# DeltaNet and gated MLP on one core: wider products in the triangular solve, later masks, another queue order and smaller first blocks in an inverse

## The chip, the cores and the metric

The kernel runs on one core of a Trainium2 chip. A core has a tensor engine (PE, matrix products into PSUM), VectorE (DVE), ScalarE (ACT), GpSimd (POOL) and SyncE (SP, which issues transfers). The metric is the device time of one execution in microseconds (us); lower is better. Times of one kernel are medians over several runs; the profile is of one further execution.

## The reference

A DeltaNet recurrence over 768 positions for 4 batches x 8 heads of width 48, and then a two-layer MLP with a sigmoid gate (384 to 2048 to 384) over the 3072 tokens:

```python
for t in range(S):
    kt, vt, bt = (k_n[:, :, t], v[:, :, t], beta[:, :, t, None])
    y[:, :, t] = np.einsum('bhd,bhde->bhe', q[:, :, t], state)
    v_old = np.einsum('bhde,bhd->bhe', state, kt)
    state = state + bt[:, :, :, None] * np.einsum('bhd,bhe->bhde', kt, vt - v_old)
...
h = x @ w_in
g = h * (1.0 / (1.0 + np.exp(-1.702 * h)))
return (g @ w_out).astype(np.float32)
```

Keys are divided by their norm first (`k_n`). The weights of the MLP arrive as 64-bit floats and are converted on the chip to 32-bit ones.

## The kernel before

**Chunks and units.** The recurrence is cut into 6 chunks of 128 positions (`C`), so that a unit is one chunk of one batch with its 8 heads: 24 units, numbered `n`, chunk by chunk. Units of different batches are independent; a chunk of a batch needs the state that the chunk before left.

**The solve in a unit.** Inside a chunk the 128 updates depend on each other through the Gram matrix G of the keys. The kernel splits the 128 rows into 4 blocks of 32 (`BS`, `NB`). `solve` multiplies the inverse of a diagonal block (XB) with the block's rows of V into psU; `solved` copies psU to the rows of U on ACT; `below` multiplies the Gram rows of the block with these U rows, for each later block of rows a product of its own (32 rows of contraction, 32 output rows, 48 columns), into psR; `rest` takes psR from the later rows of V on DVE, below block 0 in two instructions (rows 32 to 63, rows 64 to 127). Then the next block can be solved. `together` issues the products of one stage: for each head, the solves of one or two units and the belows of another, so that the chains of two or three units interleave.

**Order over the units.** Chunk 0 runs in two pairs of chains: `hops` names the stages of a pair, and the two loops over `2 * NB` stages in the kernel's end run them, with other work between: `fill(n)` converts n pieces of the MLP's weights on DVE, `preparing` (the generator `keys`) normalizes, transposes and multiplies the keys of the four units of chunk 1 and writes their diagonal blocks out, `warm` issues dense products whose results nobody reads, and `feed` issues MLP work. From chunk 1 on, `woven(n, share)` holds three stages, with unit n at blocks 1 and 2, unit n-1 at blocks 2 and 3 and unit n+1 at block 0: (solve n block 1, below n-1 block 2), (solve n-1 block 3 and n+1 block 0, below n block 1), (solve n block 2, below n+1 block 0). Between them `spend` issues MLP products (ph and po) on PE.

**Inverses.** `invert` inverts all diagonal blocks of a chunk (or of two of its batches) at once on DVE, one block per partition. It inverts two blocks of 16 rows (`HS`) inside each block of 32 by substitution, in 15 steps of one multiply and one reduction, and joins them by two products (`dots`). For chunk 0 it runs while the tensor engine prepares scores; for chunk 1 it takes turns with MLP work.

**Masks.** `select` zeroes the part of the scores M that lies on and below the diagonal, on GpSimd. For chunk 0 the four masks are issued behind the inverse's code in one loop; nothing in them waits for the inverse, so each starts when its M is there.

**Queues.** Instructions made by `vec`, `act`, `pe`, `pool`, `sync` and `other_queue` keep the order in which the program issues them on their engine. `sync` goes to SP's queue, `other_queue` to GpSimd's. In `prepare`, a unit of chunk 1 writes its four diagonal blocks to memory (Nd) and reads them back in another layout (NT), all on SP. Between the two pairs SP is also given the queries and values of units 4 and 5.

Of the kernel before, what the change touches and what calls it, by code (L numbers as in the profile page):

```python
# [18 lines left out]
def kernel(  # L19
# [274 lines left out]
    def fill(n):  # L294
        for _ in range(n):
            next(converting, None)
# [105 lines left out]
    def prepare(n):  # L402

        c, b = units[n]
        turn(n)
        yield 0.6
        G = gram(n)
        if c == 1:
            Nd = dram.tile([H * C * BS], F32, tag="Nd", name="Nd", bufs=4)
            for blk in range(NB):  # L410
                u = slice(blk * BS, (blk + 1) * BS)
                sync(out=Nd.rearrange("(h p k) -> p h k", p=C, k=BS)[u], in_=G[u, :, u])
            yield 0.9
            sync(
                out=NT[b * NB * H : (b + 1) * NB * H].rearrange("d i k -> d (i k)"),
                in_=Nd.rearrange("(d r) -> d r", r=BS * BS),
            )
            yield 0.0
            return
        Nd = dram.tile([H * NS], F32, tag="Nd", name="Nd", bufs=4)  # L420
        dma = sync if c < 3 else nc.sync.dma_start
        dma(
            out=Nd.rearrange("(h r) -> h r", r=NS)[:, 0 : C * C].rearrange(
                "h (p k) -> p h k", k=C
            ),
            in_=G,
        )
        dma(
            out=NT[b * NB * H : (b + 1) * NB * H],
            in_=Nd.rearrange("(d r) -> d r", r=NS // NB)[:, 0 : BS * C].rearrange(  # L430
                "d (i k) -> d i k", k=C
            )[:, :, 0:BS],
        )
        yield 0.9
# [6 lines left out]
    def invert(c, b0=0, nb=B):  # L441

        np = nb * NB * H
        part = slice(b0 * NB * H, b0 * NB * H + np)
        N, Y = NT[part], YB[part]
        bc = bI[part, c].broadcast_to([np, BS, BS])
        tt, red = vec.tensor_tensor, vec.tensor_reduce
        if c > 0:
            tt(N, N, bc, op=ALU.mult)
            yield 0.0  # L450
        HS = BS // 2

        def dots(o, a, b, ny, nx, nk, negate):

            P = wk.tile([128, ny, nx, nk], F32, tag="P", name="P")[part]
            tt(P, a, b, op=ALU.mult)
            red(o, P, axis=AX.X, op=ALU.add, negate=negate)

        def halves(t):

            return [t[:, s * HS : (s + 1) * HS, s * HS : (s + 1) * HS] for s in range(2)]


        Yf = Y.rearrange("p j i -> p (j i)")
        Nf = N.rearrange("p i k -> p (i k)")
        step = HS * BS + HS

        def diag(t, off, dims):
            return bass.AP(t.tensor, t.offset + off, [t.ap[0], [step, 2]] + dims)

        for i in range(1, HS):
            P = wk.tile([128, 2, i, i], F32, tag="P", name="P")[part]
            tt(
                P, diag(Nf, i * BS, [[0, i], [1, i]]), diag(Yf, 0, [[BS, i], [1, i]]),
                op=ALU.mult,
            )
            red(diag(Yf, i, [[BS, i]]), P, axis=AX.X, op=ALU.add, negate=True)
            yield 0.0


        X1 = N[:, 0:HS, HS:]
        if c <= 1:
            vec.tensor_copy(X1, halves(Y)[1].rearrange("p l i -> p i l"))
        else:
            act.activation(X1, halves(Y)[1].rearrange("p l i -> p i l"), ACT.Copy)
        A = N[:, 0:HS, 0:HS]
        N10, Y0 = N[:, HS:, 0:HS], halves(Y)[0]
        Q = 4
        for j in range(0, HS, Q):
            n = HS - j  # L490
            dots(
                A[:, j : j + Q, :],
                N10[:, :, j:].rearrange("p (o l) k -> p o l k", o=1).broadcast_to([np, Q, HS, n]),
                Y0[:, j : j + Q, j:].rearrange("p j (o k) -> p j o k", o=1).broadcast_to([np, Q, HS, n]),
                Q, HS, n, False,
            )
            yield 0.0
        for i in range(0, HS, Q):
            n = i + Q
            if c == 0 and i == HS - 3 * Q:  # L500
                warm(NY, vec.memset)
            dots(
                Y[:, 0:HS, HS + i : HS + i + Q],
                A[:, :, 0:n].rearrange("p j (o l) -> p j o l", o=1).broadcast_to([np, HS, Q, n]),
                X1[:, i : i + Q, 0:n].rearrange("p (o i) l -> p o i l", o=1).broadcast_to([np, HS, Q, n]),
                HS, Q, n, True,
            )
            yield 0.0
        if c == 0:
            T = wk.tile([128, BS, BS], F32, tag="P", name="YT")  # L510
            vec.transpose(T.rearrange("p d i -> p i d"), Y.rearrange("p j i -> p i j"))
            for b in range(B):
                XB = wk.tile([128, H, BS], F32, tag="XB", name="XB", bufs=4)
                tt(
                    XB, T[:, b * H : (b + 1) * H],
                    zs[:, 5, b].broadcast_to([128, H, BS]), op=ALU.mult,
                )
                inverse[b] = XB
                yield 0.0
            return  # L520
        YS = wk.tile([128, BS, BS], F32, tag="P", name="YS")[part]
        tt(YS, Y, bc, op=ALU.mult)
        dma = sync if c < 3 else nc.sync.dma_start
        groups = [range(b0, b0 + nb)]
        back = {}
        for bs in groups:
            for b in bs:
                back[b] = dram.tile([H * C, BS], F32, tag="Yd", name="Yd", bufs=4)
                dma(
                    out=back[b].rearrange("(p j) i -> p j i", j=BS),  # L530
                    in_=YS[(b - b0) * NB * H : (b - b0 + 1) * NB * H],
                )
            for b in bs:
                XB = wk.tile([128, H, BS], F32, tag="XB", name="XB", bufs=4)
                dma(out=XB, in_=back[b].rearrange("(h t) i -> t h i", h=H))
                inverse[c * B + b] = XB
        yield 0.0
# [7 lines left out]
    class Step:  # L545
# [63 lines left out]

        def below(self, blk, h, psR):  # L610
            r = slice(blk * BS, (blk + 1) * BS)
            for k in range(blk + 1, NB):
                u = slice(k * BS, (k + 1) * BS)
                pe.matmul(
                    psR[u, h, :], lhsT=self.G[r, h, u], rhs=self.U[r, h, :],
                    start=True, stop=True,
                )

        def rest(self, blk, psR):
            for u in (slice(BS, 2 * BS), slice(2 * BS, C)) if blk == 0 else (slice((blk + 1) * BS, C),):  # L620
                vec.tensor_tensor(self.V[u], self.V[u], psR[u], op=ALU.subtract)

        def solve(self, blk, h, psU):
            r = slice(blk * BS, (blk + 1) * BS)
# [328 lines left out]
    for s in pair:  # L953
        for h in range(H):
            act.mul(s.V[:, h, :], s.V[:, h, :], zs[:, 4, s.b, h : h + 1])
    for s in pair:
        s.select()

    def hops(a, b):
# [12 lines left out]
    def keys():  # L972

        def unit(n):
            yield from normalize_mixed(n)
            yield from prepare(n)

        begun[2 * B] = prepare(2 * B)

        def first(n):  # L980
            yield from normalize_mixed(n)
            next(begun[n])

        work = [unit(n) for n in range(B, 2 * B)] + [first(2 * B)]
        for t in range(22):
            for u, begin in enumerate((0, 3, 6, 10, 13)):
                s = t - begin
                if s >= 0 and s % 2 == 0:
                    next(work[u], None)
            yield  # L990
        for w in work:
            run(w)
# [2 lines left out]
    path = hops(*pair[:2])  # L995
    for i in range(2 * NB):
        together(*next(path))
        fill(1 if i < 2 else 2)
        if i > 0:
            ahead_of(preparing, 1)  # L1000
        warm(NU if i < 6 else NA)
    for n, s in enumerate(pair[:2]):
        put_out(s, 2 - n)
        load(len(KN) + n, ((KN, k),), other_queue)
        fill(1 + n)
    for n in range(B, B + 2):
        load(n, ((QP, q),), sync)
    for n in range(B, B + 2):
        load_values(n, sync)

    ffn = []

# [13 lines left out]
    for i in range(2 * NB):  # L1026
        together(*next(path))
        fill(2 if i < 5 else 3)
        if i > 2:
            feed()  # L1030
        else:
            warm(NU)
        ahead_of(preparing, 2)
        if 3 <= i < 6:
            fetch_out(i - 3)
    for s in pair[2:]:
        put_out(s, 2)
        feed()
        fill(1)
    ffn.append(hidden(xTs[1], gTs[1], slice(0, NTH), 1.3, True))  # L1040
    xTs.pop(0), xTs.pop(1)
    load(B + 2, ((QP, q),), sync)
    for n in range(2 * B + 1, 2 * B + 1 + HB):
        load(n, ((KN, k),), sync)
# [55 lines left out]
```

## Time and profile before

| what | us |
|---|---|
| median of 3 runs (lowest, highest) | 775.44 (774.95, 776.5) |
| the profiled execution, whole | 775.34 |
| its span in the profile | 773.6 |
| PE busy / PE weight loads busy | 747.1 / 560.1 |
| DVE / ACT / POOL busy | 455.2 / 241.5 / 126.5 |
| psU products: busy (records) | 68.6 (1536) |
| psR products: busy (records) | 60.0 (2208) |
| V minus psR on DVE: busy (instructions) | 53.3 (96) |

A product of 32-bit floats leaves two records (two passes) on PE, and weight loads are recorded apart from the products (PEld). Busy times of products that run beside each other are counted once. The mean duration of a product in the profile is its way through the pipeline (203 ns for psU and psR), not the distance to the next. The granted clock (PEclk) is the share of full speed that the tensor engine was given: 0.976 over the span. DMA and engine times in a stretch of the span are read from a table by stretch, and the order of single instructions from the timeline.

### The profile page before, as it was taken

How to read it: one execution, taken by the hardware profiler on the slowest of the kernel's cores; microseconds unless marked ns; L12 is line 12 of the kernel's file. 1: busy time of each engine (PE TensorE's matmuls, PEld its weight loads, DVE VectorE, ACT ScalarE, POOL GpSimd, SP SyncE). 2: the span in 40 equal slices, each digit the busy share in tenths (PEclk: the TensorE clock that was granted, in tenths of full speed). 3: DMA queues.
4: the chain of work that ended last, by engine and by line, in shares of the span. 5: the costliest groups of instructions: out<-in, count | busy, mean ns of one | idle time of the engine just before them, and what ended most of it. 6: DMA issues, size and time to landing. Idle time of an engine off the chain costs nothing.

```text
span 773.6 us, 18836 instructions
## 1 busy us (share of the span) xinstructions
PE 747.1 (97%) x8165; PEld 560.1 (72%) x8165; DVE 455.2 (59%) x935; ACT 241.5 (31%) x535; POOL 126.5 (16%) x132
## 2 busy tenths in 40 slices
PE   7898999789999999999999999999999999999997
PEld 6677788456688678678678678678678677686774
DVE  6989879996975675665665665666665621000000
ACT  4564642343333223223223233233223123121110
POOL 6314200010220320220221211221210000000000
PEclk8598999999999999999999999999999999999999
DMA  9946640644342142042042042042030020000000
GB/s 167 176 65 174 145 87 1 170 114 97 76 109 56 25 105 56 22 107 57 22 101 63 22 100 65 22 97 66 22 77 13 22 44 2 16 12 1 25 1 21
DMA packets 130658, 50.73 MB, mean 66 GB/s; under 512 B 105408, under 2 KB 126016, under 8 KB 130576
## 3 DMA queue, kind: packets, MB, share of 16 engines
q1 hardware_dynamic: 128112, 41.08, 24.5%
q0 software_dynamic: 2464, 8.46, 4.5%
q8 instruction: 64, 1.05, 0.6%
q14 instruction: 18, 0.15, 0.1%
HBM read 32.08 MB, written 16.25 MB: 62 GB/s over the span
## 4 chain that ended last, share of the span: by engine, by line
PE 80%; DVE 14%; issue 2%; DMA 2%; ACT 2%; SPq 0%; POOL 0%; DVEq 0%; POOLq 0%; ACTq 0%
PE po L102 29%; PE ph L102 26%; PE psY L102 6%; PE psU L102 5%; PE psQ L102 4%; PE psG L102 4%; PE psT L102 3%; DVE P L102 3%; DVE w_out L102 2%; DVE tmp L102 2%; DVE YB L102 2%; PE psR L102 2%; PE ps_warm L102 2%; DVE V L102 1%; DVE NT L102 1%
## 5 line engine op out<-in xcount | busy, mean ns | idle before, releaser
L102 PE MATMUL po<-w_out,gT 128*128 128x384 f32 x768 | 266.1, 494 | 7.4 <-DVE w_out L102 7.4
L102 PE MATMUL ph<-xT,w_in 128*128 128x256 f32 x1152 | 261.2, 383 | 0.3
L102 PEld LDWEIGHTS ph<-xT,w_in 128*128 128x128 f32 x1152 | 214.8, 190 | 32.6 <-issue 1.7
L102 PEld LDWEIGHTS po<-w_out,gT 128*128 128x128 f32 x768 | 141.1, 190 | 98.8 <-DVE w_out L102 9.1
L102 DVE TENSOR_TENSOR V<-V,psR 64x384 f32<-64x384 f32 (+1 forms) x96 | 53.3, 555 | 189.8 <-PE psR L102 186.8
L102 ACT ACTIVATE gT<-ph 128x512 f32<-128x512 f32 x96 | 56.5, 596 | 142.3 <-PE ph L102 142.2
L102 DVE TENSOR_TENSOR P<-NT,YB 64x8 f32<-64x8 f32 (+31 forms) x190 | 89.4, 470 | 5.4
L102 ACT COPY US<-psU 32x384 f32<-32x384 f32 x92 | 43.2, 470 | 134.7 <-PE psR L102 120.5
L102 DVE TENSOR_REDUCE YB<-P 64x4 f32<-64x8 f32 (+31 forms) x190 | 80.9, 426 | 6.5
L102 PEld LDWEIGHTS psU<-V,XB 32*32 32x32 f32 x1536 | 57.7, 105 | 36.5 <-issue 27.7
L102 PE MATMUL psU<-V,XB 32*32 32x48 f32 x1536 | 68.6, 203 | 3.2 <-DVE V L102 2.4
L605 POOL TENSOR_SCALAR_AFFINE_SELECT M<-M 128x1024 f32<-128x1024 f32 x20 | 25.4, 1268 | 231.4 <-DVE M L102 167.4
L102 PE MATMUL psR<-US,G 32*32 32x48 f32 x2208 | 60.0, 203 | 0.6 <-ACT US L102 0.6
L102 PEld LDWEIGHTS psR<-US,G 32*32 32x32 f32 x2208 | 50.7, 105 | 1.9 <-ACT US L102 0.7
L102 PE MATMUL psQ<-QS,kT 48*128 48x176 f32 (+1 forms) x384 | 37.6, 341 | 3.0 <-ACT QS L102 3.0
L102 PE MATMUL psG<-kT 48*128 48x128 f32 x384 | 32.4, 306 | 3.4 <-ACT kT L102 2.2
L102 PEld LDWEIGHTS psQ<-QS,kT 48*128 48x128 f32 x384 | 31.1, 209 | 6.2 <-ACT QS L102 5.1
L102 DVE TENSOR_TENSOR P<-NT 64x256 f32<-64x256 f32 (+7 forms) x40 | 34.3, 859 | 0.4
L102 DVE TENSOR_REDUCE NT<-P 64x64 f32<-64x1024 f32 (+7 forms) x40 | 32.6, 815 | 1.4
L102 PEld LDWEIGHTS psG<-kT 48*128 48x128 f32 x384 | 27.4, 205 | 6.8 <-ACT kT L102 2.6
L102 ACT COPY o<-po 128x384 f32<-128x384 f32 x24 | 11.5, 479 | 61.7 <-issue 39.2
L102 ACT COPY M<-psQ 128x256 f32<-128x256 f32 x68 | 22.8, 376 | 22.7 <-DVE V L102 16.0
(99 smaller groups left out, 600.9 us busy)
## 6 DMA issues: line engine op xcount, KB each, us to landing
Nd<-G SPq DMA_DIRECT2D x16, 512.0 KB, 3.5
QP<-in_q_dram SPq DMA_DIRECT2D x24, 192.0 KB, 4.3
V<-in_v_dram SPq DMA_DIRECT2D x24, 192.0 KB, 3.1
out_dram<-o SPq DMA_DIRECT2D x24, 192.0 KB, 2.6
KN<-in_k_dram POOLq DMA_DIRECT2D x15, 192.0 KB, 3.6
NT<-Nd SPq DMA_DIRECT2D x20, 128.0 KB, 2.6
Yd<-YS SPq DMA_DIRECT2D x20, 128.0 KB, 2.4
XB<-Yd SPq DMA_DIRECT2D x20, 128.0 KB, 3.3
```

Of the source, the lines that this page charges most:

```text
L102: return lambda *a, **kw: tc.keep_in_program_order(op(*a, **kw))
L605: (pool if self.n < B else nc.gpsimd).affine_select(out=self.M, in_=self.M, compare_op=ALU.is_gt, fill=0.0, base=0, pattern=[[0, H], [1, 1 ...
```

## The change

- `below`: one product for all rows below a block instead of one for each block of 32. Below block 0 it runs over all 128 output rows, below block 1 over rows 64 to 127, below block 2 over rows 96 to 127. `rest` is one subtraction over the same rows; below block 0 it also changes the rows of block 0 itself, which are not read again.
- `invert`: for chunks 0 and 1 the substitution goes over four blocks of 8 rows (7 steps), and pairs of them are joined by four `dots` of 8 x 8 x 8 after one copy.
- Masks of chunk 0: a copy on GpSimd that reads the last column of YB, which the inverse writes last, stands ahead of them; the first two masks follow it, and the other two are issued in the first pair's loop after stages 3 and 5.
- SyncE's order: an extra `yield` between the writes of Nd and the read of NT; `keys` steps the later units first, in 24 turns instead of 22; the queries and values of units 4 and 5 are loaded in the second pair's loop (stage 5) and behind it, no longer ahead of it. In the first two stages `fill` converts two pieces instead of one.

```diff
             for blk in range(NB):
                 u = slice(blk * BS, (blk + 1) * BS)
                 sync(out=Nd.rearrange("(h p k) -> p h k", p=C, k=BS)[u], in_=G[u, :, u])
+            yield 0.0
             yield 0.9
             sync(
                 out=NT[b * NB * H : (b + 1) * NB * H].rearrange("d i k -> d (i k)"),
...
-        for i in range(1, HS):
-            P = wk.tile([128, 2, i, i], F32, tag="P", name="P")[part]
+        for i in range(1, QS):
+            P = wk.tile([128, nb8, i, i], F32, tag="P", name="P")[part]
...
+        if QS < HS:
+            shape = [np, QS, QS, QS]
+            first, second = ([slice(s * HS + o, s * HS + o + QS) for s in range(2)] for o in (0, QS))
+            vec.tensor_copy(
+                diag(Nf, QS, [[BS, QS], [1, QS]], 2), diag(Yf, QS * BS + QS, [[1, QS], [BS, QS]], 2)
+            )
+            for a, b in zip(first, second):
+                dots(
+                    N[:, a, a],
...
+            for a, b in zip(first, second):
+                dots(
+                    Y[:, a, b],
...
         def below(self, blk, h, psR):
             r = slice(blk * BS, (blk + 1) * BS)
-            for k in range(blk + 1, NB):
-                u = slice(k * BS, (k + 1) * BS)
-                pe.matmul(
-                    psR[u, h, :], lhsT=self.G[r, h, u], rhs=self.U[r, h, :],
-                    start=True, stop=True,
-                )
+            u = self.under(blk)
+            pe.matmul(
+                psR[u, h, :], lhsT=self.G[r, h, u], rhs=self.U[r, h, :],
+                start=True, stop=True,
+            )
+
+        def under(self, blk):
+
+            return slice((blk + 1) * BS if blk else 0, C)
 
         def rest(self, blk, psR):
-            for u in (slice(BS, 2 * BS), slice(2 * BS, C)) if blk == 0 else (slice((blk + 1) * BS, C),):
-                vec.tensor_tensor(self.V[u], self.V[u], psR[u], op=ALU.subtract)
+            u = self.under(blk)
+            vec.tensor_tensor(self.V[u], self.V[u], psR[u], op=ALU.subtract)
...
-    for s in pair:
+    pool.tensor_copy(landed, YB[:, 0, BS - 1 : BS])
+    for s in pair[:HB]:
         s.select()
...
-        for t in range(22):
-            for u, begin in enumerate((0, 3, 6, 10, 13)):
+        for t in range(24):
+            for u, begin in reversed(list(enumerate((0, 3, 6, 10, 13)))):
...
-        fill(1 if i < 2 else 2)
+        fill(2)
+        if i in (3, 5):
+            pair[HB + (i - 3) // 2].select()
...
-    for n in range(B, B + 2):
-        load(n, ((QP, q),), sync)
-    for n in range(B, B + 2):
-        load_values(n, sync)
...
+        if i == 5:
+            load(B, ((QP, q),), sync)
+            load_values(B, sync)
...
+    load(B + 1, ((QP, q),), sync)
+    load_values(B + 1, sync)
```

## The prediction

> **What bounds the kernel now.** I read the slices of the span first, then the busy time by stretch, then the chain that ended last.
>
> ```profile
> PE   7898999789999999999999999999999999999997
> ...
> PEclk8598999999999999999999999999999999999999
> ...
> PE 80%; DVE 14%; issue 2%; DMA 2%; ACT 2%; SPq 0%; POOL 0%; DVEq 0%; POOLq 0%; ACTq 0%
> ```
>
> The tensor engine (PE) is full at full clock from slice 10 on and carries 80% of the chain; VectorE (DVE) carries 14%, all before 180 us.
>
> ```profile
> 44.00:64.00 20.00, 16.91 (x394) 13.77 (x395) 17.89 (x30) 8.59 (x19) 1.85 (x2) 0.92 0.28 51
> ...
> 120.00:180.00 60.00, 50.72 (x390) 33.83 (x389) 53.83 (x102) 20.97 (x41) 4.87 (x3) 0.97 0.41 104
> 180.00:774.00 594.00, 588.17 (x6202) 436.27 (x6200) 301.14 (x629) 160.03 (x353) 85.60 (x68) 1.00 0.20 48
> ```
>
> Columns: stretch, length, busy PE, PE weight loads, DVE, ScalarE, GpSimd, granted clock, DMA share, GB/s. From 180 us on PE is busy 588 of 594 us and DVE only 301: there a microsecond more of PE is a microsecond more of time, and one less of DVE is worth nothing. DVE is near its limit only between 44 and 180 us. So I price each edit on PE first.
>
> **How a stage of small products runs.** Weight loads around one `together` of chunk 1 (start, duration, engine, operation):
>
> ```profile
> 285.84 0.62 PEld L102 LDWEIGHTS ph<-xT,w_in 128*128 128x128 f32 x3
> 286.79 0.11 PEld L102 LDWEIGHTS psU<-V,XB 32*32 32x32 f32 x2 [0.33 <-issue]
> 286.81 0.11 PEld L102 LDWEIGHTS psR<-US,G 32*32 32x32 f32 x2
> ...
> 287.43 0.11 PEld L102 LDWEIGHTS psR<-US,G 32*32 32x32 f32 x2
> 287.61 0.51 PEld L102 LDWEIGHTS ph<-xT,w_in 128*128 128x128 f32 x3
> ```
>
> From 286.79 to 287.52 lie 8 heads, each with two passes (an f32 product is two records) of two psU and two psR. One pass of all four takes 42 ns (0.68 us over 16), just the stream of 48 columns; and a stage with one psU and three psR has the same period (294.79 to 295.39 us). The four run beside each other, each in its own 32x32 square: two of three psR cost nothing today.
>
> Around the stage the shape changes. The last ph of 128x128 starts at 286.487 and streams 213 ns, to 286.700; the next load waits until 286.794. At the far end the last psR starts at 287.478 and streams to 287.518; ph's load waits until 287.607. So 94 and 89 ns of nothing, and then a load that lies beside no product. I read the same gap at all 264 places of the trace where the shape changes: at least 89 to 110 ns for each of 16 pairs of shapes, also where the rows stay and only the columns change (psD 64x32 to psG 64x128: 94 ns). Between equal shapes there is none.
>
> **The Trainium skill.** "TensorEngine Tiling (Array Packing)", Key Properties, says that different tiles run in parallel and that "Changing tiling mode (not just tile) drains the TensorE", 32x32, 32x64 and 32x128 being different modes: the trace agrees, with those gaps. "TensorE: Matmul & The Clock Gate", LDWEIGHTS, has a load cost its columns over 1.2, whatever the rows: agreed, 48-column products on 64-column weights come every 58 ns (297.214 to 297.272), not every 42; so a 128-column load is about 107 ns. Its Part 1 says that the clock falls to half after a 3.4 us window with too little work; see below. "GPSIMD Engine Reference", Specifications: SBUF access shared with VectorE for instructions with two SBUF inputs.
>
> ```profile
> 33.49 0.42 DVE L102 TENSOR_TENSOR P<-NT,YB 128x256 f32<-128x256 f32 x1
> ...
> 34.19 1.09 POOL L102 TENSOR_SCALAR_AFFINE_SELECT M<-M 128x1024 f32<-128x1024 f32 x1 [1.97 <-ACT M L102]
> 34.40 1.16 DVE L102 TENSOR_TENSOR P<-NT 128x256 f32<-128x256 f32 x1
> ```
>
> It agrees once in four masks: the multiply took 1.16 us beside a mask, 0.42 alone.
>
> **The change part by part.**
>
> *One product.* Below block 0 it is 32x128 (rows 0 to 127, the first 32 unused), below block 1 32x64, below block 2 32x32 as before. `together` still alternates solve and below head by head, so wherever below 0 or 1 meets a solve, the shape changes twice a head. The trace has no 32x32 next to 32x128; I price by the gaps above. psU: gap 94, load 27, two passes 84: 205 ns. 32x128: gap 90, load 107, pass 42, and the second load, overlapping that pass, ends 107 after the first; pass 42: 347 ns. Head 552 ns, stage 4.42 us against 0.68: +3.7. 32x64: gap 90, two loads of 53 and a pass of 42: 238 to 248 ns, head 0.45 to 0.46 us, stage about 3.7 us: +3.0. In `woven`, below 1 meets solves in 20 steps and below 0 in 19; the first below 0 is alone (16 loads of 107 ns: +1.0). 19 x 3.7 + 1 + 20 x 3.0 = **+132 us**, all where PE is the bound. Chunk 0 has 4 + 4 such stages in its two pairs of chains, 27 us; PE idles 9 us between 120 and 180 us, some of which takes this up: **+20**.
>
> *The clock.* Windows of 3.41 us, and the one after each:
>
> ```profile
> 57.41:60.82 3.41, 1.90 (x41) 1.24 (x38) 3.28 (x7) 1.41 (x2) 0.00 (x0) 1.00 0.00 0
> 60.83:64.23 3.40, 2.74 (x22) 2.45 (x23) 3.34 (x6) 0.47 (x1) 0.40 (x1) 0.50 0.94 224
> 135.91:139.32 3.41, 1.67 (x5) 0.82 (x6) 3.31 (x8) 1.36 (x3) 1.91 (x1) 1.00 0.86 186
> 139.33:142.73 3.40, 2.62 (x8) 1.20 (x8) 3.26 (x8) 0.61 (x1) 0.00 (x0) 1.00 1.02 229
> 170.05:173.46 3.41, 1.90 (x78) 1.43 (x78) 3.31 (x9) 1.57 (x3) 0.00 (x0) 1.00 0.02 5
> 173.47:176.87 3.40, 3.40 (x14) 1.91 (x11) 2.18 (x5) 1.09 (x2) 0.00 (x0) 0.50 0.15 45
> ```
>
> The clock (third number from the end) halved after the first and third, not after the second, which had less busy time but full-size products. Weighted by rows times columns over 128 squared, streaming fills about 0.24, 0.39 and 0.23 of the three windows; no window at full clock that kept it, from 44 us on, was below 0.39. In a new stage a head streams 168 of 450 to 550 ns on a sixteenth to a quarter of the array: 0.05. A window with more than 2.5 us of such a stage falls under 0.3; by the free position of windows that is 85% of the 4.4 us stages and 64% of the 3.7 us ones, some 28 of 39. Each costs half a window (1.7 us) or, where the rest of the stage keeps the next window cold too, 3.4: I take 3, +84, and +9 in chunk 0. If the gate counts otherwise, nothing; both ends are kept.
>
> *One subtraction below block 0* removes 24 DVE instructions of 555 ns (widths 32 and 64 both take 555, so 128 should). Twenty lie behind PE; four are in the stretch where DVE is tight: -2. The next solve waits for an instruction as long as before.
>
> *Blocks of 8 rows.* The fifteen steps of the first inverse take 16.61 to 27.52, 10.9 us. Seven steps on twice the blocks (durations at 4, 16, 36 ... 196 elements from this list, 0.16 to 0.37, and 45 ns between) are 4.0; a copy about 0.35; four pairs at 512 elements (0.68 + 0.69 + gaps) 5.8: 10.15. **-0.7** in the first inverse, as much in the second.
>
> *Masks.* GpSimd's four leave the inverse: -0.7 (the one collision). Behind the new wait on YB stand only GpSimd's powers and the loads of keys and weights on its queue, the first at 55.34 us in the trace, the inverse being done at 41.6; two masks now stand between hops, and may cost a collision each.
>
> *SyncE's order and the extra yield.* Two QP and two V loads leave the queue ahead of the Nd writes (73 to 80 us) and an NT read no longer stands directly behind its own writes (SP waited 12.9 us on Nd, seven times). The second inverse began at 107.27; it could begin up to 6 us earlier, but with PE some 13 us late before it nothing of that shows: 0. The later loads are first used after the chunk-0 outputs. Two conversion pieces more in the first hops: DVE idles there once PE is slow: 0.
>
> **Sum.** The profiled execution is 775.3 us (span 773.6 and 1.7 around it), the runs' median 775.4: the same. 775.4 + 132 + 20 - 4 = 923; with the clock, + 93 = 1016.
>
> **Rivals.**
> - *A drain without the clock's fall*: 923, own range 880 to 955. For it: my weighting rests on three falls. Chance 0.30.
> - *No drain between shapes of 32 rows; loads bind*: below 0 takes 16 x 112 = 1.8 us, below 1 16 x 58 = 0.93: 20 x (1.1 + 0.25) = 27, chunk 0 some 3, DVE and queues -6: 799. For it: no such pair in the trace. Against: 264 changes of 264. Chance 0.09.
> - *Faster*: loads of one row group are pulled ahead and the stages stay at 0.68 us; the first phase keeps -4, and up to -6 of the queue: 768. It decides only while a stage grows by less than 7/39 = 0.18 us, which one pair of gaps exceeds. Chance 0.05; no change 0.01.
> - *Worse than 1085*: cold windows follow each other, 0.05.
>
> **How the numbers follow.** Likeliest is drain and clock, 0.50: 1016, rounded to 1015; own range 955 to 1085. The range 880 to 1085 holds it and the first rival, 0.80. Within 0.2% of 775.4 a measurement can't tell a change: faster 0.05, same 0.01, slower 0.94.
>
> **What would show it.** psR groups of 32x128 and 32x64; in `woven`, psU and psR alternating about every 0.25 us and stages of 3.7 to 4.4 us; PEclk digits under 9 past slice 10. Stages near 1.8 us would mean no drain; 0.7, that my main term is wrong. The first inverse should start its last transposition some 1.4 us earlier.

## The result, and the profile after

The changed kernel takes 1005.34 us (1004.13 to 1007.62, 4 runs) against 775.81: a ratio of 1.296, 95% interval 1.293 to 1.299. Its profiled execution took 1006.41 us, span 1004.7. In two experiments below, the grouped order (869 to 892 us) and the small filler (928 to 950 us), the four runs spread by over 2% at different clocks; their ratios use the two faster ones, and the profile of the small filler is of a longer one.

The slices of the span and the chain by engine, as shown of the kernel before:

```profile
PE   7999999899999999999999999999999999999998
...
PEclk7658689988899889889997997999979889978999
...
PE 95%; DVE 2%; ACT 1%; issue 1%; POOL 0%; POOLq 0%; ACTq 0%; DVEq 0%
```

PE is as full as before, but its clock is under 90% of full speed in 20 of the 40 slices (before in 3), and nearly the whole chain is PE. DVE's 14% went to 2%: its waits for psR grew from 187 to 386 us. The busy times by stretch (columns as in the prediction):

```profile
44.00:64.00 20.00, 20.00 (x128) 14.55 (x125) 5.82 (x8) 4.79 (x12) 0.00 (x0) 0.68 0.20 24
...
120.00:180.00 60.00, 59.06 (x409) 49.78 (x408) 44.25 (x77) 20.10 (x41) 4.74 (x5) 0.91 0.34 70
```

Between 44 and 64 us, where DVE had 17.9 us of work, it now has 5.8, and PE left 128 records where it had left 394, partly at half clock (0.68 here). The groups of small products:

```profile
L102 PE MATMUL psR<-US,G 32*64 32x48 f32 (+2 forms) x1104 | 167.4, 259 | 0.0
L102 PE MATMUL psU<-V,XB 32*32 32x48 f32 x1536 | 136.5, 218 | 0.4 <-DVE V L102 0.3
```

Half the psR products take 167 us of PE instead of 60, and the psU products, which the change did not touch, 137 instead of 69. The columns that stream did not become more; the products stopped lying side by side, and part of them ran at half clock. The timeline of PE in a stage with 32x128 at full clock:

```profile
386.68 0.81 PE L102 MATMUL ph<-xT,w_in 128*128 128x256 f32 x3
387.42 0.27 PE L102 MATMUL psU<-V,XB 32*32 32x48 f32 x2
387.62 0.42 PE L102 MATMUL psR<-US,G 32*128 32x48 f32 x2
387.97 0.27 PE L102 MATMUL psU<-V,XB 32*32 32x48 f32 x2
388.16 0.42 PE L102 MATMUL psR<-US,G 32*128 32x48 f32 x2
```

One head is 387.42 to 387.97: 0.545 us, in which psU has 0.20 and the wide psR 0.35. Eight of them are a stage of 4.35 us, up to the start of the next product; the stages with 32x64 and two solves take 3.55. Before, both took 0.81. The gap in front of each 32x128 load is 89 ns after the last psU pass has streamed. Such a gap, with the weight load behind it that lies beside no product, is called a drain below. The shape changes 969 times in this trace, 264 times in the one before.

### The profile page after: what moved, and what is told of

Its sections match the earlier page's. It is cut to its first block, busy times and chain, and to the rows that moved or that the text cites. A ratio compares the mean times of both kernels' runs of the same rounds, so it can differ in the third digit from the quotient of the medians.

```text
span 1004.7 us, 16489 instructions
## 1 busy us (share of the span) xinstructions
PE 987.1 (98%) x7013; PEld 733.1 (73%) x7013; DVE 438.0 (44%) x897; ACT 241.1 (24%) x535; POOL 127.0 (13%) x133
## 4 chain that ended last, share of the span: by engine, by line
PE 95%; DVE 2%; ACT 1%; issue 1%; POOL 0%; POOLq 0%; ACTq 0%; DVEq 0%
PE po L102 27%; PE ph L102 26%; PE psR L102 13%; PE psU L102 10%; PE psY L102 7%; PE psG L102 4%; PE psQ L102 4%; PE ps_warm L102 3%; PE psT L102 3%; DVE w_out L102 1%; DVE tmp L102 0%; DVE P L102 0%; DVE YB L102 0%; ACT QS L102 0%; PE psD L102 0%
## 5 line engine op out<-in xcount | busy, mean ns | idle before, releaser
L102 PE MATMUL po<-w_out,gT 128*128 128x384 f32 x768 | 285.8, 524 | 4.0 <-DVE w_out L102 3.9
L102 PE MATMUL ph<-xT,w_in 128*128 128x256 f32 x1152 | 275.8, 398 | 0.3
L102 DVE TENSOR_TENSOR V<-V,psR 128x384 f32<-128x384 f32 (+2 forms) x72 | 40.1, 557 | 398.3 <-PE psR L102 385.7
L102 PE MATMUL psR<-US,G 32*64 32x48 f32 (+2 forms) x1104 | 167.4, 259 | 0.0
L102 PE MATMUL psU<-V,XB 32*32 32x48 f32 x1536 | 136.5, 218 | 0.4 <-DVE V L102 0.3
L102 PEld LDWEIGHTS psR<-US,G 32*64 32x64 f32 (+2 forms) x1104 | 116.4, 154 | 28.0 <-ACT G L102 0.5
L102 PEld LDWEIGHTS psU<-V,XB 32*32 32x32 f32 x1536 | 77.6, 108 | 54.5 <-issue 28.9
L102 DVE TENSOR_TENSOR P<-NT,YB 64x8 f32<-64x8 f32 (+26 forms) x178 | 84.2, 473 | 4.9
L102 DVE TENSOR_REDUCE YB<-P 64x4 f32<-64x8 f32 (+27 forms) x178 | 77.2, 434 | 6.1
L628 POOL TENSOR_SCALAR_AFFINE_SELECT M<-M 128x1024 f32<-128x1024 f32 x20 | 24.5, 1227 | 279.7 <-DVE M L102 209.7
L102 PE MATMUL psY<-M,US 128*64 128x128 f32 x368 | 39.3, 383 | 0.0
```

Of the source, the lines that this page charges most:

```text
L102: return lambda *a, **kw: tc.keep_in_program_order(op(*a, **kw))
L628: (pool if self.n < B else nc.gpsimd).affine_select(out=self.M, in_=self.M, compare_op=ALU.is_gt, fill=0.0, base=0, pattern=[[0, H], [1, 1 ...
```

## The experiments

**Which edit carries it.** The product and its subtraction alone, in the kernel before:

```diff
-            for k in range(blk + 1, NB):
-                u = slice(k * BS, (k + 1) * BS)
-                pe.matmul(psR[u, h, :], ...)
+            u = self.under(blk)
+            pe.matmul(psR[u, h, :], ...)
```

> The kernel before with the one product and the one subtraction alone. Theory (drains at each change of shape, and the clock's fall that they bring): it carries the whole change, 775.8 + about 233 = 1005 to 1012 us, a granted clock near 0.87. Rival (a good part comes from the other three edits, such as the queue order or the waiting masks): clearly less, under 980 us.

1007.03 us (1003.99 to 1012.13), ratio 1.297 (1.291 to 1.303), clock 0.871. And the changed kernel with that edit taken back:

> The changed kernel with the products and the two subtractions of before, so the other three edits alone. Theory: 768 to 774 us, a gain of 2 to 8 us, since VectorE's work and the queue's waits before 180 us shrink. Rival (these edits cost time too): over 777 us.

775.54 us (22 runs), ratio 0.9989 (0.9976 to 1.0002). So the one product is the whole slowdown. The other three edits bring at most 1.9 us by the interval, which holds no change too; the expected 2 to 8 us did not come.

**Drains, or the wide products themselves.** The changed kernel with the stage in another order:

```diff
         for h in range(H):
             for X, blk in solves:
                 X.solve(blk, h, psU)
+        for h in range(H):
             for X, blk in belows:
                 X.below(blk, h, psR)
```

> The changed kernel, but a stage issues all its solves first and then all its wide products, so that the shape changes twice in a stage and not sixteen times. Theory (the drains carry the cost): a stage with 32x128 lasts 0.68 + 16 x 0.112 + 0.2 = 2.7 us, one with 32x64 0.68 + 16 x 0.058 + 0.2 = 1.8 us, against 4.35 and 3.55; over before 19 x 1.9 + 1.1 + 20 x 1.0 = 57 us and 12 us in chunk 0, hardly a fall of the clock: 835 to 855 us. Rival (the wide products themselves, their loads or their share of PSUM, carry it): no better than 990 us.

Ratio 1.119 (1.115 to 1.124), 869 us. PE's timeline in a stage of each kind:

```profile
315.63 0.87 PE L102 MATMUL psU<-V,XB 32*32 32x48 f32 x32
316.43 1.13 PE L102 MATMUL psR<-US,G 32*64 32x48 f32 x16
...
324.60 0.86 PE L102 MATMUL psU<-V,XB 32*32 32x48 f32 x16
325.39 1.98 PE L102 MATMUL psR<-US,G 32*128 32x48 f32 x16
327.30 1.09 PE L102 MATMUL psY<-QS,ST 48*64 48x128 f32 x16
```

The stages last 1.85 and 2.70 us as expected (324.60 to 327.30), with the same wide products: 136 us of the slowdown are the alternation and what it does to the clock, not the width. The total missed its range by 14 us. Two things had been left out: the stages of 32x32 alone lost their overlap too (1.33 us instead of 0.80 in 23 stages, 12 us), and 13 falls of the clock past 180 us remained, each of one window of 3.41 us, which is up to 22 us.

**The clock without drains.** The kernel before, with products added at the head of each stage that the change widens, in one case small, in the other full-size:

```diff
+        def idle(self, blk, psR):
+            for _ in range((44, 36)[blk] if blk < 2 and self.n >= B else 0):
+                pe.matmul(
+                    psR[0:BS, 0, :], lhsT=self.G[0:BS, 0, 0:BS], rhs=self.U[0:BS, 0, :],
+                    start=True, stop=True,
+                )
...
+        for X, blk in belows if solves else ():
+            X.idle(blk, psR)
         for h in range(H):
```

> The kernel before, with 44 (36) products of 32x32 by 48 columns more at the start of each woven stage that the change widens below block 0 (block 1), written into rows that nobody reads: the tensor engine streams without a break and without a change of shape for 3.7 (3.0) us more. Added products: 19 x 3.7 + 20 x 3.0 = 130 us. If the clock's gate weighs work by the share of the array in use: falls as in the changed kernel, 985 to 1015 us, clock under 0.92. If it counts busy time alone: no falls, 906 us, clock 0.97.

Ratio 1.2015 (1.192 to 1.211), about 932 us: between the two expected cases. The clock was 0.926 in the profile (span 945.2) and 0.948 in the fastest run. A window of 3.4 us of the profile and the next, and what PE ran in the first:

```profile
310.57:313.97 3.40, 3.40 (x127) 3.40 (x128) 0.00 (x0) 0.00 (x0) 0.00 (x0) 1.00 0.02 5
313.99:317.38 3.39, 3.39 (x64) 2.94 (x53) 1.11 (x2) 0.47 (x1) 0.00 (x0) 0.50 0.02 5
...
309.76 3.79 PE L102 MATMUL psR<-US,G 32*32 32x48 f32 x85
```

PE was busy for all 3.40 us, with 32x32 products only, and its clock was halved right after. It fell 24 times past 180 us.

```diff
+            ps = psR.rearrange("p h d -> p (h d)")[:, 0:256]
+            for _ in range((34, 28)[blk] if blk < 2 and self.n >= B else 0):
+                pe.matmul(ps, lhsT=ones[:, 0:128], rhs=ones, start=True, stop=True)
```

> The same stages, lengthened by 34 (28) bf16 products of 128x128 by 256 columns, overwritten later: 3.6 (3.0) us and one change of shape of about 0.2 us, together 19 x 3.8 + 20 x 3.2 = 137 us. Both theories: the clock stays at 0.97 and the time is 910 to 918 us; a fall here would mean that something else than idle array lets the clock fall.

900.23 us, ratio 1.159 (1.155 to 1.164), clock 0.982. By stretch, the small filler's kernel and then the full-size one's:

```profile
180.00:945.00 765.00, 760.43 (x9263) 598.28 (x9259) 303.25 (x631) 163.38 (x360) 87.09 (x68) 0.94 0.16 39
```

```profile
180.00:898.00 718.00, 713.30 (x7348) 548.64 (x7347) 302.29 (x629) 160.18 (x354) 87.08 (x68) 1.00 0.17 41
```

Stages of nearly the same length (4.46 and 3.85 us small, 4.62 and 3.96 full-size): the clock falls with small products and stays with full-size ones. The fillers differ in type too (f32 and bf16), but the full-size ph and po of the MLP are f32, and the clock stayed up over 594 us of the kernel before that are mostly ph and po.

So the gate of the clock does not go by busy time. A weight by the share of the array in use, as in the prediction (rows times columns over 128 squared, times the streaming time), fits. I estimate the streaming time at 0.83 ns a column and pass for f32 (213 ns for the 256 columns of a ph) and half of that for bf16 (the full-size filler's products of 256 columns come every 109 ns). Of the whole windows of 3.41 us at full clock past 40 us in six traces (before, after, the product alone, the grouped order and the two fillers), 123 were followed by half speed and had a share of at most 0.38; the other 1227 had at least 0.29. A limit of 0.315 errs in 9 of the 1350. By streaming time alone the best limit errs in 42: windows at 0.95 fell, and one at 0.39 did not. The page that the prediction cites here, Part 1 of "TensorE: Matmul & The Clock Gate", speaks of an idle window; the window shown above was not idle, and the measurement decides.

The time of the small filler lies between my two cases, since its stages bring fewer and shorter falls: in the changed kernel 15 of the 32 falls past 180 us lasted two windows or more, here 3 of 24. The full-size one came in 10 us under its range. By 186 us about 4 us of that had come, as longer stages of chunk 1 took the place of PE's waits for converted weights; another 4 came in small steps over the later stages, and the rest is not traced.

**The other edits, one by one.** Products of 32x32 with the one subtraction, and the other three edits:

```diff
-            u = self.under(blk)
-            pe.matmul(psR[u, h, :], ...)
+            for k in range(blk + 1 if blk else 0, NB):
+                u = slice(k * BS, (k + 1) * BS)
+                pe.matmul(psR[u, h, :], ...)
```

> The changed kernel with products of 32x32 again, four of them below block 0 (its own rows too, so that the one subtraction over 128 rows reads what was written), and the one subtraction. Theory: the fourth product lies in a square of its own beside the others in the woven stages and costs nothing; with the other three edits 773 to 776 us, a granted clock over 0.96. Rival (the subtraction over 128 rows, or the wait for it, has its part in the slowdown): over 780 us.

774.26 us (22 runs), ratio 0.9968 (0.9952 to 0.9984): 0.3% faster than the kernel before. The subtraction is no part of the slowdown. One miss inside: the fourth product is not free, its stages take 0.89 us instead of 0.81; why stays open. The subtraction alone, in the kernel before:

> The kernel before with one subtraction below block 0 over 128 rows and a fourth 32x32 product there, nothing else. Theory: four instructions of 555 ns less on VectorE between 44 and 95 us, where it is near its limit; in chunk 0 the fourth product shares a square with a solve in some stages, 0.1 us each: 773 to 776 us. Rival (VectorE's time there is hidden as it is from 180 us on): 775.5 to 777 us.

775.12 us, ratio 0.9985 (0.9971 to 0.9999): on the side of the gain, but the interval all but reaches no change. The blocks of 8 rows alone:

> The kernel before with the blocks of 8 rows in the first two inverses alone. Theory: each inverse is 1 to 2 us shorter on VectorE, but the first solve waits for the tensor engine's filler products (until about 44 us) and gains nothing; 774.5 to 776.5 us. Rival (it was on the path that sets the end): 772 to 774 us.

774.99 us, 0.9985 (0.9974 to 0.9995), in the expected range, with the first solve at 44.38 us. DVE's timeline beside three of the four masks of GpSimd, and one of these masks:

```profile
30.67 1.47 DVE L102 TENSOR_TENSOR P<-NT,YB 128x512 f32<-128x512 f32 x1
...
34.49 1.47 DVE L102 TENSOR_TENSOR P<-NT 128x512 f32<-128x512 f32 x1
...
38.45 1.86 DVE L102 TENSOR_TENSOR P<-NT 128x1024 f32<-128x1024 f32 x1
...
30.51 1.09 POOL L102 TENSOR_SCALAR_AFFINE_SELECT M<-M 128x1024 f32<-128x1024 f32 x1 [1.90 <-ACT M L102]
```

Three multiplies took 0.64 to 0.79 us longer than their like (0.68 and 1.22 us), where the trace before has one such collision, and the last transposition started at 41.59 instead of 41.66. The shorter inverse is not shown to be the reason: the profiles of the product alone and of the small filler, with the longer inverse, have three such collisions too. The masks alone:

```diff
+    pool.tensor_copy(landed, YB[:, 0, BS - 1 : BS])
-    for s in pair:
+    for s in pair[:HB]:
         s.select()
...
+        if i in (3, 5):
+            pair[HB + (i - 3) // 2].select()
```

> The kernel before with the masks of chunk 0 behind the inverse alone. Theory from the other runs: the inverse loses one collision of 0.7 us, but the masks then stand beside the multiplies that make XB (2.50 us instead of 1.43 in the run of the other three edits), so the first solve is not earlier: 775.5 to 777 us. Rival (the gain of 0.7 us arrives): under 775.3 us.

775.86 us, 0.9992 (0.9974 to 1.001): as expected, no change that can be told. The queue's order alone (the edits of the diff in `prepare`, `keys`, the loads and `fill`):

> The kernel before with SyncE's order, the extra yield and the two more conversion pieces alone. Theory as in the prediction: the second inverse may begin up to 6 us earlier once the tensor engine is not late; of that at most 3 us reach the end, since the conversions of the weights bound that stretch: 772.5 to 776 us. Rival (later queries and values delay unit 4): over 776.5 us.

776.55 us, 1.0000 (0.9983 to 1.0016): the expected gain did not come, and whether the rival's small loss is there can't be told. The second inverse did begin earlier, at 105.45 us instead of 107.27. Last, less filler ahead of the first solve in the fastest version:

```diff
-    NW, NA, NY, NU = 14, 3, 46, 11
+    NW, NA, NY, NU = 14, 3, 30, 11
```

> The fastest version so far (small products, one subtraction, the other three edits) with 30 instead of 46 filler products ahead of the first solve, which the shorter inverse now ends before. If the filler is the last wait before the first solve: 1 to 2 us less, 771.5 to 773.5 us. Rival (without them the window is not full enough and the clock rises 3.4 us later): 774 to 778 us.

775.83 us, 1.0001 (0.9986 to 1.0015), as the rival had it. In the profiles, one of each, the first solve came at 42.35 instead of 43.20 us, but the second pair began at 69.15 instead of 67.43: a low-clock window fell at 47.3 us in the first pair's hops, which it had not done with 46. With the filler the kernel is faster (ratio 0.9968); that this window is the reason is likely, but one profile of each doesn't show it.

## Why the prediction was right

1. *Two of three psR cost nothing, so one product saves nothing on PE.* Held: a stage of four products per head and pass and one of two had been equally long, and halving the products made the stages longer.
2. *Every change of shape drains.* This was inferred from other pairs of shapes, and holds for 32x32 next to 32x64 and 32x128: 89 ns ahead of the wide load. The heads were put at 552 and 450 to 460 ns (the terms of the second add up to 443 to 453) and took 545 and 444; the stages at 4.42 and 3.7 us and took 4.35 and 3.55. With the 0.81 us that a stage really takes before (the prediction's 0.68 left out the time from its last pass to the next product), the woven stages are 19 x 3.54 + 1.1 + 20 x 2.74 = 123 us at full clock, where I had 132.
3. *The clock falls.* Held: 32 falls past 180 us, without the one at the very end, where I had counted 28. PE's busy time and granted clock up to the last solve of the second pair of chains, and from there to the end, first before:

```profile
0.00:92.41 92.41, 80.66 (x1378) 66.18 (x1378) 77.86 (x154) 48.73 (x117) 34.42 (x59) 0.82 0.80 149
92.41:773.64 681.23, 666.48 (x6789) 493.90 (x6788) 377.29 (x782) 192.73 (x419) 92.10 (x73) 1.00 0.23 54
```

   and after:

```profile
0.00:136.19 136.19, 127.98 (x1185) 97.40 (x1185) 75.67 (x145) 49.18 (x118) 33.46 (x60) 0.67 0.55 99
136.19:1004.69 868.50, 859.10 (x5829) 635.73 (x5828) 362.30 (x753) 191.92 (x418) 93.52 (x73) 0.91 0.18 43
```

   PE's busy time grew by 47.3 and 192.6 us, and its idle time fell by 3.5 and 5.4. At full clock the drains are 25 us in the first part (4 x 3.54 + 4 x 2.74) and 123 in the second. By subtraction the clock has 22 and 70, together 92; I had 9 and 84, together 93. This is a remainder, not measured by itself, but its size fits: a clock of 0.875 over 1004.7 us is 251 us at half speed, and 0.976 over 773.6 us was 37, so 214 more, half of which is 107. The cost is lower in part because about 60 us of the half speed lie in the widened stages themselves, where a 32x128 head takes 0.88 us, 1.6 times 0.545 and not twice.
4. *Chunk 0: the term that was mis-sized.* I had put its drains at 27 us, let PE's idle time take up 7 of them and given the clock 9: 29 together. The last solve of the second pair came at 136.19 instead of 92.41 us: 44 later, with 25 of drains, 3.5 taken up and 22 of the clock, which was at half speed from 51.1 to 81.8 us without a break. The woven part came out smaller: about 187 us, of which 123 are drains, 70 the clock, less 5.4 of idle time, against 132 + 84. So the sum of the drains was 11 us too high. That the clock's total came out so close is luck: the two parts miss by 13 and 14 us in opposite directions.
5. *The other three edits, -4.* Measured -0.9 by the ratio, with an interval from -1.9 to +0.2: too much hope, and by a failing step. The last transposition did start earlier, by 2.25 us (39.41 against 41.66) and not by 1.4, since blocks of 8 rows took 9.43 us to the copy of the halves instead of 10.15. But the first solve came at 44.17 against 44.20. Ahead of it PE works off its filler products until about 44 us, and behind the inverse three masks ran beside the multiplies that make XB, which took 2.48 us instead of 1.43. The third of them is issued after stage 3, but nothing stood before it on GpSimd, so it ran right behind the first two, where the prediction had it between the hops. The filler stands nowhere in the prediction. The earlier second inverse showed in the traces (102.19 us in the fastest version against 107.27), but alone the queue's order brought no time.

Rivals: no drain between shapes of 32 rows is refuted by the gaps and by the stages of 4.35 us; a drain without the clock's fall (923 us) by the clock of 0.875; the faster one with both. That the gate weighs the share of the array was an argument from few falls; the two fillers show that small products alone let it fall, and the 1350 windows that the share tells the two kinds apart better than streaming time does.

## What to carry to other kernels

Before merging small matrix products, see whether they run beside each other: if the stage's length is one stream, the merged ones were free, and a merged product of another shape forbids the overlap with its neighbours. Keep one tile shape within an interleaved stage, or group by shape; count the changes of shape, at about 0.1 us and an uncovered weight load each. And count low array use as idle time of the clock's gate: here stretches of 3 to 4 us of small products were often followed by 3.4 us or more at half clock, which the large products behind them paid for.

## What the runs showed of the hardware that was not expected

- A tensor engine that was busy for a whole 3.4 us window, with 32x32 products only, had its clock halved (the small filler, 310.57 to 317.38 us). In the six traces the share of the array in use told such windows from others at about 0.3.
- A drained head is 1.6 times as long at half clock (0.88 against 0.545 us), not twice.
- Where a GpSimd mask and a VectorE multiply with two inputs from SBUF overlapped by over 0.2 us in the traces, the one that had started second took longer than alone, by the overlap less about 0.14 us, and the first did not. In the run of the shorter inverse alone the three multiplies above started second, while the mask of 26.70 us, behind a multiply that started at 26.43, took 1.90 us instead of 1.09. The trace before has a mask of 1.84 us at 30.38 too, which the prediction's "once in four masks" left out.
